# Score and state parts of two tiles in one 64-row visit, one-bank PSUM tiles, and a new fixed order of instructions

## The chip, the cores and the metric

The kernel runs on one core of one Trainium2 chip. The time of a kernel is its device time in microseconds (us); a program is run several times, and the median counts. The kernel before took 214.94 us (median of three runs, 214.93 to 215.87).

## What is computed

Inputs are q, k, v with 4 batches, 8 heads, 768 positions and head size 64, a gain vector of 512, and two weight matrices (512 x 2048 and 2048 x 512). The first part is a recurrence per batch and head; the second a normalised two-layer network with a residual:

```python
for t in range(S):
    state = gamma[None, :, None, None] * state + np.einsum('bhd,bhe->bhde', k[:, :, t], v[:, :, t])
    y[:, :, t] = scale * np.einsum('bhd,bhde->bhe', q[:, :, t], state)
...
mu = np.mean(x, axis=-1, keepdims=True)
var = np.mean((x - mu) ** 2, axis=-1, keepdims=True)
xn = (x - mu) / np.sqrt(var + 1e-06) * g_ln
ch = np.maximum(xn @ w_ch1, 0.0) @ w_ch2
return (x + ch).astype(np.float32)
```

Here x is y with the heads side by side, so one position has 8 x 64 = 512 features.

## The kernel before, in words

**Tiles.** The work is cut into 24 tiles of 128 positions. Tiles 0 to 3 are the first chunks of the four batches; tiles 4 to 8 are chunks 1 to 5 of batch 0, tiles 9 to 13 those of batch 1, and so on. Per tile the recurrence is done in chunk form. The steps, with their names in the code:

- Loads `k`, `q`, `v`: GpSimd (POOL) issues them with a cast to bf16 (L430). From tile 8 (`T0 = 8`) q and k lie side by side in one buffer.
- Before tile 8, TensorE (PE) transposes k and q with an identity (L498, L505), 4 instructions each, ScalarE (ACT) copies kT out (`ek`) and VectorE (DVE) scales qT (`eq`, L510). From tile 8, one DMA transpose issued by SyncE (SP) turns q and k together (`tr`, L520), and DVE scales qT (L527).
- Scores `pa` (L538): 8 matmuls that contract over 64 rows of the array, for the 8 heads, even heads on rows 0 to 63 and odd heads on rows 64 to 127. They write `pa`, one tile over two PSUM banks.
- DVE multiplies the scores by the decay mask (`asb`, L562) in one instruction of 1024 columns.
- The state part: q times the state of earlier chunks. For tiles 4 to 7 it is 4 full-height matmuls (L582) inside `py`; from tile 8 it is 8 matmuls of 64 rows (`ps`, L548), which come just before the tile's scores. Scores and state parts together are a "visit" of the array in 64-row form.
- `py` (L572, L586): 8 matmuls of masked scores times v. From tile 8 even and odd heads go to two banks, b1 and b2.
- The state: POOL scales v (`vg`, L633), PE multiplies kT by it into bank `pd` (L645), DVE scales the result into one of two state buffers (`pb`, L659).
- DVE takes mean and variance (`bn`, L601), normalises (`xn`, L613), ACT keeps a copy of y (`xc`, L619). xn is transposed on PE for tiles 0 to 7 (`tx`, L672, copied out by ACT as `ex`) and by a DMA transpose on SP from tile 8 (`ex`, L686).
- Network: `m` (L719) is a first-layer unit with 512 PSUM columns; groups have 1 tile (tiles 0 to 7), 2 tiles (8 to 15) or 4 tiles (16 to 23), so a matmul has 128, 256 or 512 columns. `r` is the relu that empties it, on ACT (L732) or DVE (L734). A unit uses one of two `mm` banks. The second layer (L757, "m2") takes 16 matmuls of 512 columns per tile in a bank b0, b1 or b2; DVE adds the residual (L767) and ACT issues the store (L774).

**PSUM.** Eight banks: `pd` 1, `mm` 2, `pa` 2, b0, b1, b2.

**Order.** No scheduler runs at compile time: `ORDER` (L29) is a list of task numbers written out by hand, and `Plan.order` walks it, so each engine's queue has exactly this order. Every engine takes its queue in order, and waits at an instruction whose inputs, or whose buffer, aren't ready. A plan's cost figures (the `a(...)` calls) only place filler matmuls on zeros (`warm`, L785) in the first 14 us. POOL's queue also holds small copies (L447), which wait for an earlier load to land and so pace the loads.

Of the kernel before, what the change touches and what calls it, by code (L numbers as in the profile page):

```python
# [14 lines left out]
PE, ACT, DVE, POOL, SP = range(5)  # L15

CFG = {
    "T0": 8, "TX": 8, "groups": [1] * 8 + [2] * 4 + [4] * 2,
    "first": ["iota", "pos", "v0", "k1", "q1", "v1", "w1_0", "k2", "q2", "w1_1", "v2",
              "k3", "q3", "v3", "w1_2", "k4", "q4", "v4", "k5", "q5", "v5", "w1_3", "w2_0",  # L20
              "k6", "q6", "v6", "k7", "q7", "v7", "w2_1", "w2_2", "w2_3"],
    "bufs": {"qsb": 6, "ksb": 5, "vsb": 9, "qk": 8, "tr": 6, "vg": 3, "trq": 3, "trk": 3},
    "load_pad": 600, "w_pad": 550, "lead": 32, "lead2": 32, "sq_at": 28000, "late_load": 1700, "two": 4, "m2b": ("b0",), "m2all": 16, "inter": 4, "every": 4, "tail": (0, 384, 512), "step": 8, "pace": 8, "ahead": 3,
    "slack": 600, "tr_pad": 4000, "x_pad": 3500, "vg_pad": 2500, "fill": 0.8, "fill_end": 14000,
}

ORDER = [int(x) for x in """  # L29
16 17 2 0 3 19 20 23 14 8 15 1 24 5 7 9 25 4 10 6 13 21 11 26 18 45 22 27 146 28 149  # L30
100147 148 150 46 29 151 30 162 100163 153 12 152 165 154 164 166 155 31 156 157 167 32
158 168 169 47 100176 159 170 524 177 178 160 179 100172 214 180 181 171 173 532 33 215
182 183 525 184 534 161 190 533 193 34 35 36 526 100191 186 535 192 194 10527 187 540 37
38 185 542 195 48 196 49 39 541 216 197 204 40 42 43 41 536 198 50 217 543 207 234
100205 206 528 537 200 52 51 201 544 199 208 10529 224 209 545 552 188 548 10549 553 174
100225 210 227 550 551 546 53 55 175 226 228 211 54 212 44 218 219 547 213 554 530 220
555 251 202 221 235 100241 229 538 230 56 244 10531 236 556 539 242 275 231 558 100258
557 232 559 243 560 10561 237 562 57 245 246 233 238 239 563 222 566 259 564 247 260 567
248 189 261 570 262 252 565 568 249 60 254 255 250 569 223 253 203 263 100722 61 268 58
59 62 287 298 63 723 716 724 301 66 67 64 717 65 264 725 269 718 571 719 265 726 266 270  # L40
720 576 100271 276 307 267 578 272 579 577 728 273 68 69 278 277 72 729 730 731 318 73
279 70 299 71 280 580 572 732 281 300 282 74 322 284 286 734 735 75 288 581 283 285 736
302 303 290 289 573 737 291 738 574 319 584 292 740 741 293 320 294 296 742 308 304 240
585 78 575 743 582 744 295 297 310 333 79 76 309 77 339 586 305 583 311 80 746 587 334
747 312 335 313 314 274 316 323 81 315 748 84 350 749 351 588 592 317 325 85 82 83 379
750 589 256 257 324 354 326 727 602 86 752 87 753 327 328 329 603 593 590 754 755 594
591 330 90 331 340 352 332 342 756 341 343 721 380 598 321 599 595 91 758 336 759 344
760 761 596 733 88 345 89 355 762 346 368 348 353 600 92 757 745 739 337 597 347 93 764
96 349 97 94 381 601 95 765 98 338 357 604 356 766 606 386 99 605 382 607 767 358 306
359 383 614 612 768 360 384 615 361 613 363 770 397 102 771 103 100 362 772 398 365 364  # L50
763 369 101 104 371 370 773 403 610 372 608 774 611 373 776 616 609 399 366 105 374 387
108 109 617 375 618 414 367 377 106 107 777 620 418 751 376 378 389 619 110 388 778 390
779 622 415 391 385 404 780 392 393 621 623 630 782 395 111 114 429 115 631 394 112 400
456 113 433 626 116 624 117 396 406 120 121 416 405 430 783 627 625 407 784 431 408 628
419 409 634 785 410 629 632 411 412 457 118 119 122 413 421 635 786 445 633 420 123 788
126 458 422 127 789 646 124 423 424 790 425 427 647 401 125 426 428 791 642 638 434 436
792 435 794 795 796 639 643 465 769 437 438 640 417 439 440 442 128 797 459 641 129 441
446 443 476 132 644 798 432 402 133 645 636 130 448 447 648 131 134 138 637 460 650 449
450 649 800 651 461 451 452 801 802 477 454 803 444 775 480 462 453 466 478 455 135 491
804 136 137 468 492 467 806 139 495 807 469 470 140 493 808 471 141 809 472 142 474 473  # L60
475 652 653 654 481 483 482 484 810 655 656 658 143 510 479 485 144 787 506 805 657 799
145 659 660 661 486 662 507 496 487 489 664 663 488 508 490 666 498 497 665 499 667 668
670 669 500 671 501 502 672 673 504 511 812 674 503 505 676 513 512 675 514 678 463 677
680 515 679 682 813 681 814 683 516 494 811 509 517 781 519 464 518 520 815 100830 831
816 521 832 818 819 200824 820 825 684 817 793 685 826 690 688 691 827 689 694 696 833
695 522 686 697 687 708 709 821 698 699 692 693 523 822 848 700 828 834 702 100842 701
703 706 707 704 200836 714 837 705 715 712 838 849 843 713 710 711 850 844 845 839 846
851 840 100854 852 855 856 823 847 841 835 829 853 857 860 861 858 862 863 864 859 865
""".split()]


class Plan:

    def __init__(self, seen, begin, first_load):
        self.seen, self.begin, self.first_load = seen, begin, first_load  # L80
        self.tasks, self.bufs, self.chosen = [], {}, {}

    def pool(self, name, n):
        self.bufs[name] = n

    def add(self, eng, ns, rank, emit, after=(), takes=None, uses=(), load=0, hw=0, lat=0, at=0,
            follows=(), slack=0, slots=None):
        after = [d for x in after for d in (x if isinstance(x, list) else [x])]
        t = {"on": eng if isinstance(eng, dict) else {eng: ns}, "rank": rank, "emit": emit,
             "after": after, "takes": takes, "uses": list(uses) + ([takes] if takes else []),  # L90
             "slots": (slots or [(takes[0],)]) if takes else [],
             "load": load, "hw": hw, "lat": lat, "at": at, "follows": list(follows),
             "slack": slack}
        self.tasks.append(t)
        return t

    def order(self, seq):
        left, ends = {}, {}
        for t in self.tasks:
            for u in t["uses"]:  # L100
                left[u] = left.get(u, 0) + 1
        held = {name: [] for name in self.bufs}
        free = dict(self.begin)
        sw_free, hw_free, out = self.first_load, 0, []
        for number in seq:
            t = self.tasks[number % 10000]
# [55 lines left out]
def kernel(  # L162
# [9 lines left out]
):  # L172

    nc = tc.nc
# [641 lines left out]
```

## Time and profile before

| what | value |
|---|---|
| median time, 3 runs | 214.94 us |
| span of the profiled execution | 212.1 us |
| own time of the profiled execution | not given apart; the median is 2.9 us above its span |
| PE busy | 204.2 us (96%) |
| DVE, ACT, POOL busy | 121.6, 85.0, 95.8 us |
| granted TensorE clock | 1.000 |

The span runs from the first to the last instruction of the profiled execution; launch and end lie around it. Matmuls are pipelined: the duration that a row gives one matmul holds its way through the array, so the rate is read from the starts of rows, not from durations. A timeline row gives start, length, engine, line, what is written and read, shape and how many.

### The profile page before, as it was taken

Reading aid. Unit: us, or ns where it says so; the run is one execution under the profiler, and the core shown is the slowest. Engines: PE = TensorE matmul, PEld = TensorE weight load, DVE = VectorE, ACT = ScalarE, POOL = GpSimd, SP = SyncE. Lnnn points to the kernel's source line nnn. Section 1 sums busy time; section 2 is a strip of 40 time slices with the busy share of each in tenths; the row PEclk is TensorE's granted clock in tenths of the full one; section 3 lists DMA queues with packets and bytes.
Section 4 is the critical chain, followed back from the end, with each engine's and each line's share of the span. In section 5 each row is a group of like instructions: output and inputs, shape, how many; then the busy total and the mean of one; then the engine's idle time right before and its main releaser. Section 6 shows DMA issues by size and latency. Waiting matters only on the chain.

```text
span 212.1 us, 4939 instructions
## 1 busy us (share of the span) xinstructions
PE 204.2 (96%) x2005; PEld 130.8 (62%) x2027; DVE 121.6 (57%) x264; ACT 85.0 (40%) x173; POOL 95.8 (45%) x149
## 2 busy tenths in 40 slices
PE   7988999999999999999999999999999999999993
PEld 3468999975667666657576676574444444444442
DVE  6776778674566875664775777478676510030041
ACT  5485556750431323332352442351366601444200
POOL 8988697238776584657855837430000000000000
PEclk9999999999999999999999999999999999999999
DMA  9999999999999999999999999959440260000035
GB/s 130 174 180 180 163 198 173 208 139 114 112 100 93 155 119 177 168 269 145 134 145 181 105 173 84 157 83 151 86 157 10 65 185 3 0 0 0 0 141 209
DMA packets 108890, 26.85 MB, mean 127 GB/s; under 512 B 101569, under 2 KB 105921, under 8 KB 108866
## 3 DMA queue, kind: packets, MB, share of 16 engines
q0 software_dynamic: 77024, 13.37, 83.7%
q1 hardware_dynamic: 27186, 6.59, 21.1%
q10 hardware_dynamic: 4656, 6.56, 9.0%
q8 instruction: 16, 0.26, 0.5%
q14 instruction: 8, 0.07, 0.1%
HBM read 27.30 MB, written 6.29 MB: 158 GB/s over the span
## 4 chain that ended last, share of the span: by engine, by line
PE 87%; DMA 8%; POOL 3%; issue 1%; DVE 0%; POOLq 0%
PE b L757 39%; PE mm L719 38%; DMA ksb<-in_k_dram 4%; DMA w<-in_moe_w_ch_dram 3%; PE pa L538 2%; PE pd L645 2%; PE b L572 2%; PE b L548 2%; POOL v L430 1%; PE b L498 1%; PE b L672 1%; POOL vg L633 0%; PE b L586 0%; PE b L582 0%; PE b L505 0%
## 5 line engine op out<-in xcount | busy, mean ns | idle before, releaser
L719 PE MATMUL mm<-xnt,w 128*128 128x128 bf16 (+2 forms) x896 | 95.5, 257 | 0.2 <-ACT xnt L256 0.2
L757 PE MATMUL b<-w,h 128*128 128x512 bf16 (+2 forms) x379 | 88.4, 370 | 1.2 <-issue 0.2
L732 ACT ACTIVATE h<-mm 128x512 bf16<-128x512 f32 x91 | 53.8, 599 | 81.4 <-PE mm L719 81.1
L719 PEld LDWEIGHTS <-w 128*128 128x128 bf16 x896 | 66.0, 98 | 20.5 <-issue 0.2
L757 PEld LDWEIGHTS <-h 128*128 128x128 bf16 x400 | 37.1, 98 | 37.7
L562 DVE TENSOR_TENSOR asb<-pa,mask 128x1024 bf16<-128x1024 f32 x24 | 29.4, 1224 | 19.9 <-PE pa L538 19.7
L767 DVE SCALAR_TENSOR_TENSOR osb<-b,rstd,x_all 128x512 f32<-128x512 f32 (+2 forms) x25 | 18.0, 726 | 25.9 <-PE b L757 25.6
L601 DVE BATCH_NORM_STATS2 bns<-b 128x6 f32<-128x256 f32 (+1 forms) x40 | 17.8, 477 | 17.7 <-PE b L572 10.9
L619 ACT CAST x_all<-b 128x256 bf16<-128x256 f32 (+1 forms) x40 | 16.2, 416 | 22.5 <-DVE xn L613 20.3
L613 DVE SCALAR_TENSOR_TENSOR xn<-b,mv,gb 128x256 bf16<-128x256 f32 (+1 forms) x40 | 20.1, 532 | 0.7
L633 POOL TENSOR_TENSOR vg<-vsb,vsc 128x512 bf16<-128x512 bf16 x16 | 16.6, 1044 | 6.7 <-PE pd L645 5.9
L430 POOL DMA_DIRECT2D vsb<-in_v_dram x20 | 18.0, 901 | 2.7 <-issue 1.6
L659 DVE TENSOR_TENSOR state<-pd,gch 64x256 bf16<-64x256 f32 x40 | 16.6, 415 | 4.1 <-PE pd L645 3.2
L430 POOL DMA_DIRECT2D qk<-in_k_dram x16 | 14.3, 892 | 2.6 <-issue 2.0
L430 POOL DMA_DIRECT2D qk<-in_q_dram x16 | 14.2, 890 | 0.7 <-issue 0.7
L447 POOL COPY scrap<-qk 1x1 bf16<-1x1 bf16 x30 | 5.4, 181 | 13.4 <-DMA qk<-in_k_dram 11.7
L447 POOL COPY scrap<-vsb 1x1 bf16<-1x1 bf16 x15 | 2.6, 177 | 16.4 <-DMA vsb<-in_v_dram 16.3
L700 DVE RECIPROCAL rstd<-rstd 128x1 f32<-128x1 f32 (+2 forms) x14 | 2.2, 157 | 12.9 <-ACT rstd L694 12.8
L785 PE MATMUL pd<-zeros 128*128 128x512 bf16 (+1 forms) x24 | 6.6, 420 | 1.3 <-DVE zeros L291 1.2
L438 POOL DMA_DIRECT2D w<-in_moe_w_ch_dram x8 | 6.2, 776 | 3.0 <-DMA w<-in_moe_w_ch_dram 3.0
L572 PEld LDWEIGHTS <-asb 128*128 128x128 bf16 x128 | 5.8, 98 | 2.4
L527 DVE TENSOR_TENSOR trq<-tr,qsc 128x512 bf16<-128x512 bf16 x16 | 6.9, 432 | 0.0
(68 smaller groups left out, 127.9 us busy)
## 6 DMA issues: line engine op xcount, KB each, us to landing
out_dram<-osb ACTq DMA_DIRECT2D x23, 256.0 KB, 3.2
w<-in_moe_w_ch_dram POOLq DMA_DIRECT2D x8, 512.0 KB, 10.0
vsb<-in_v_dram POOLq DMA_DIRECT2D x20, 128.0 KB, 5.4
qk<-in_k_dram POOLq DMA_DIRECT2D x16, 128.0 KB, 4.7
qk<-in_q_dram POOLq DMA_DIRECT2D x16, 128.0 KB, 4.9
qsb<-in_q_dram POOLq DMA_DIRECT2D x7, 128.0 KB, 9.1
v<-in_v_dram POOLq DMA_DIRECT2D x4, 128.0 KB, 7.0
ksb<-in_k_dram POOLq DMA_DIRECT2D x4, 128.0 KB, 9.5
```

The source lines that it names most:

```text
L430: nc.gpsimd.dma_start(out=tile_of(kind, j), in_=src)
L562: nc.vector.tensor_tensor(out=take("asb", t, [P, NPAIR, 2, P], BF16).rearrange("p i a t -> p a i t"), in0=held["pa", t], in1=mask.rearrang ...
L572: nc.tensor.matmul(half_y[h % 2][:, h // 2 * D:(h // 2 + 1) * D], lhsT=held["asb", t][:, h // 2, h % 2, :], rhs=tile_of("v", t)[:, h, :], ...
L601: nc.vector.bn_stats(out=bns[:, t, i, :], in_=x)
L613: nc.vector.scalar_tensor_tensor(out=dst, in0=src, scalar=mv[:, t, 0:1], in1=g, op0=ALU.subtract, op1=ALU.mult)
L619: nc.scalar.copy(out=dst, in_=src)
L633: e.tensor_tensor(out=take("vg", j, [P, H, D], BF16), in0=tile_of("v", j), in1=vsc[:, cc, :].unsqueeze(2).to_broadcast([P, H, D]), op=ALU. ...
L659: nc.vector.tensor_tensor(out=held["pb", n][o, :, o], in0=held["pd", b][o, :, o], in1=gch[o, cc, :].unsqueeze(2).to_broadcast([D, NPAIR, D ...
L719: nc.tensor.matmul(p[:, j, :], lhsT=w1[:, ko, (ho + j) * P:(ho + j + 1) * P], rhs=held["xnt", hb][:, h0:h0 + n, ko, :], start=(ko == 0), s ...
L732: nc.scalar.activation(out=dst, in_=src, func=AF.Relu)
L757: nc.tensor.matmul(held[key][:, 0:w], lhsT=held["h1", hb][:, ho, i * P:(i + 1) * P], rhs=w2[:, ho, cols], start=(ho == 0), stop=(ho == HO ...
L767: nc.vector.scalar_tensor_tensor(out=take("osb", key, [P, w], FP32), in0=held[key][:, 0:w], scalar=rstd[:, t:t + 1], in1=x_all[:, t, cols] ...
```

## The change

The kernel is written anew around the same steps; the order is now a list of named tokens. A token is a step and its tile (`eq8`, `py8`), for `m` and `r` a group and its first hidden block (`m8_0`), for `z` (second layer) a tile and a quarter (`z3_2`); after a slash stand the engine, and after a second one the PSUM banks. `vis8` is the visit of tiles 8 and 9; `am9b` is the mask product of tile 9's odd heads; `gk9` and the like are POOL's pacing copies, `W` and `Z` the weight loads, `ad` and `st` residual and store.

- From tile 8 on, tiles go in pairs: one visit holds the scores of both tiles, 16 matmuls, and then the state parts of both, 16 matmuls. There are 8 visits instead of 16 there.
- PSUM is eight one-bank tiles: X0 to X3 shared by first-layer units and scores (a pair takes all four), Y0 and Y1 for even and odd heads of the pair's y, M for transposes and second-layer tiles, PD for the state. Near the end second-layer tiles also use Y0, Y1 and PD.
- The mask product is one DVE instruction per bank (512 columns), two for each tile.
- `T0` goes from 8 to 6: tiles 6 and 7 are transposed by DMA, and their state parts are done in 64 rows.
- Three state buffers instead of two; a second-layer quarter waits for its own quarter of w2 only.
- A new order throughout. The matmul of the gain vector (`gb`) now precedes tile 0's transposes; more of the early relus are on DVE.

```diff
-    "T0": 8, "TX": 8, "groups": [1] * 8 + [2] * 4 + [4] * 2,
+CFG = {'T0': 6,
+ 'pairs': [(8, 9), (10, 11), (12, 13), (14, 15), (16, 17), (18, 19), (20, 21), (22, 23)],
...
-            ("pd", 1, ps), ("mm", 2, ps), ("pa", 1, ps),
-    BANKS = ("b0", "b1", "b2")
+    BANK = {name: ps.tile([P, 4 * P], FP32, name=name)
+            for name in ("X0", "X1", "X2", "X3", "Y0", "Y1", "M", "PD")}
...
-            for i in range(NPAIR):
-                for par in range(2):
-                    o = slice(D * par, D * (par + 1))
-                    nc.tensor.matmul(
-                        half_y[par][:, i * D:(i + 1) * D], lhsT=held["trq", t][o, i, :],
-                        rhs=held["pb", t][o, i, o], start=(i == 0), stop=False)
+    def _(eng, first):
+        ts = visit[first]
+        for t in ts:
+            for i in range(NPAIR):
+                for par in range(2):
+                    o = slice(D * par, D * (par + 1))
+                    nc.tensor.matmul(bank(("pa", t, par))[:, i * P:(i + 1) * P], lhsT=kT(t)[o, i, :],
+                                     rhs=slot(trq, t)[o, i, :], start=True, stop=True)
+        for t in ts:
+            for i in range(NPAIR if t >= T0 else 0):
+                for par in range(2):
+                    o = slice(D * par, D * (par + 1))
+                    nc.tensor.matmul(
+                        y_of(t, par)[:, i * D:(i + 1) * D], lhsT=slot(trq, t)[o, i, :],
+                        rhs=slot(state, chunk(t) - 1)[o, i, o], start=(i == 0 and t == ts[0]), stop=False,
+                        skip_group_check=True)
...
-                out=take("asb", t, [P, NPAIR, 2, P], BF16).rearrange("p i a t -> p a i t"),
-                in0=held["pa", t],
-                in1=mask.rearrange("p (i a) t -> p a i t", a=2), op=ALU.mult)
+            out=slot(asb, t)[:, :, par, :], in0=bank(("pa", t, par)).rearrange("p (i t) -> p i t", t=P),
+            in1=mask.rearrange("p (i a) t -> p a i t", a=2)[:, par], op=ALU.mult)
...
+m2_12//X2 tr7 m4_12//X3 tx5//Y1 m1_12//X0 r2_12/D gq8 ex5 xc5 v7 Z1 m4_4//X2 r4_12/A eq6 Z2 vg6
+m5_0//X1 z1_0//M r4_4/A r1_12/A Z3 vis6//X3,X2 r5_0/A m5_8//X0 am6a am6b k8 pd6 m4_0//X3 q9 py6
...
+tr8 bn7 xn7b xn7a gv8 k9 vg1 xc7a xc7b r6_0/A sq6 r6_8/A r6_12/A q10 z2_0//Y0 z0_0//Y1 z2_1 v9
+pb8 r4_8/D ad1 rs0 rs2 tx7//M tr9 gk9 k10 ex7 pd1 z0_1 m7_0//X0 z2_2 z2_3 z0_2 gq10 q11 gv9 v10
+vg9 tr10 z0_3 z3_0//M ad2 eq8 pb9 ad0 gk10 k11 r7_0/A sq5 z3_1 eq9 gq11 gv10 pd9
+vis8//X2,X1,X3,X0 v11 q12 z3_2 am9b am9a am8a z3_3 tr11 gk11 k12 ad3 gv11 am8b py9 m6_4//X0
+m7_4//X3 py8 vg10 st3/A r7_4/A gq12 r6_4/A q13 z4_0//M v12 z4_1 rs4 pb10 bn8 rs5 bn9 z4_2 xn9a
+xn8b z4_3 xc8b gk12 ad4 k13 pd10 gv12 vg11 rs6 xn8a xn9b pb11 eq10 eq11 ex9 m7_8//X3 m7_12//X0
+z5_0//M v13 xc9a r7_8/A r7_12/A sq7 xc8a xc9b z5_1 ex8 gk13 vg12 vis10//X1,X2,X3,X0 gq13 k14
+tr12 z5_2 am11a am11b z5_3 tr13 gv13 q14 vg2 v14 py11 pd11 am10b ad5 m8_0//X2 z6_0//M bn11 am10a
...
```

## Prediction

> **What bounds the kernel now.** I read the page's busy table first, then the chain of work that ended last, then a timeline of TensorE alone. The page:
>
> ```profile
> PE 204.2 (96%) x2005; PEld 130.8 (62%) x2027; DVE 121.6 (57%) x264; ACT 85.0 (40%) x173; POOL 95.8 (45%) x149
> PEclk9999999999999999999999999999999999999999
> PE 87%; DMA 8%; POOL 3%; issue 1%; DVE 0%; POOLq 0%
> ```
>
> TensorE is busy all the time at full clock, and the chain is TensorE's own queue for 87% of the span; the DMA and POOL shares belong to the start, where loads gate the first tiles. The busy time by stretch of the steady part says the same (columns: stretch, PE, PEld, DVE, ACT, POOL busy, clock, DMA share, GB/s):
>
> ```profile
> 24.00:206.00 182.00, 180.79 (x1734) 114.71 (x1753) 102.61 (x211) 70.89 (x145) 75.63 (x121) 1.00 1.09 119
> ```
>
> From 24 us on, 180.8 of 182 us are covered. I also compared the start of each matmul with the one before: after 23.2 us nearly every matmul starts one streaming time after its predecessor (0.056, 0.109 or 0.216 us for 128, 256, 512 columns), bar records that the trace lost, one pause of 0.2 us at 97 us, and the visits in 64-row form. One visit, in the timeline of TensorE:
>
> ```profile
> 131.04 1.91 PE L719 MATMUL mm<-xnt,w 128*128 128x256 bf16 x16
> 132.88 0.29 PE L548 MATMUL b<-state,trq 64*128 64x64 bf16 x8
> 133.01 0.39 PE L538 MATMUL pa<-trq,tr 64*128 64x128 bf16 x8
> 133.33 2.76 PE L757 MATMUL b<-w,h 128*128 128x512 bf16 x11
> 135.93 0.40 PE L572 MATMUL b<-vsb,asb 128*128 128x64 bf16 x8
> 136.16 1.04 PE L719 MATMUL mm<-xnt,w 128*128 128x256 bf16 x8
> 137.03 1.03 PE L757 MATMUL b<-w,h 128*128 128x512 bf16 x4
> ```
>
> The 8 matmuls from 136.16 to 137.03 take 0.87 us, 0.109 each. At that rate the 16 from 131.04 are through at 132.78, but the visit starts at 132.88: 0.10 us is lost on entry. The 8 scores take 0.32 us to the next start; even and odd heads overlap, so they stream 4 x 128 columns, 4 x 0.056 = 0.22 us: 0.10 us is lost on leaving. **So one visit costs about 0.2 us beyond its work.** Everything that TensorE no longer does is time won, if nothing arrives late.
>
> **The Trainium skill.** "TensorEngine Tiling (Array Packing)", Key Properties, says that a change of tiling mode drains the TensorEngine. The two pauses of 0.10 us are that; the page has no price. "TensorE: Matmul & The Clock Gate", Back-to-back issue gap, gives N/2.4 + 2.5 ns warm: 56, 109 and 216 ns, as here. "PSUM — Partial Sum Buffer", in its section on bank collisions, says to guard PSUM by bank and quadrant: a mask product per bank frees each bank alone, but scores in a bank keep first-layer units out of it; no run here shows the mixed use. "DMA: Bandwidth & Descriptors", Queues, rings and completion order, says that the DMA engines go round their queues packet by packet: transposes and loads take from each other. The trace agrees: score transposes land 3.0 to 7.0 us after issue, later while loads are dense.
>
> **The change part by part,** against the profiled execution: span 212.1 us; its own time isn't given, and the median is 2.9 us above the span. I leave that as it is.
>
> Removed from TensorE, all on the bounding queue:
>
> ```profile
> 28.97 0.39 PE L505 MATMUL b<-idn,qsb 128*128 128x128 bf16 x4
> 29.20 0.39 PE L582 MATMUL b<-state,trq 128*128 128x128 bf16 x4
> 29.42 0.40 PE L586 MATMUL b<-vsb,asb 128*128 128x64 bf16 x8
> ```
>
> 1. Transposes of q and k of tiles 6 and 7: 4 groups of 4; a group takes 29.20 - 28.97 = 0.23 us. **-0.9 us.**
> 2. State parts of tiles 6 and 7: full-height 0.22 us (29.42 - 29.20), in 64 rows 0.13 us (133.01 - 132.88), inside visits that exist anyway: 2 x 0.09, **-0.2 us.**
> 3. Eight visits fewer, 0.2 us each: **-1.6 us.** Bounds: 0.1 us each if only entry or leaving is saved (-0.8), and 0.25 if the small 64-row work also packs better over two tiles (-2.0). I take 0.2, since a merged visit has one entry and one leaving.
>
> Sum -2.7; with roundings I take **-2.6 us.** All other matmuls keep number and shape.
>
> Edits that I cost at nothing, with their cover. **Mask product per bank:** 48 of 512 columns for 24 of 1024 (1224 ns). The nearest row is VectorE's relu of 512 columns, 687 ns; below, half of the old, 612. That is 0 to 3.6 us more on VectorE, busy 57%. For a pair of tiles it has about 4 x 0.65 mask, 2 x 0.75 residual, 4 x 0.42 state, 4 x 0.48 normalising, 4 x 0.42 + 2 x 0.21 statistics, 2 x 0.43 scaling, 10.6 us by these durations (they overlap by nearly 0.1 when back to back: about 9) in 11 to 14 us of TensorE work from visit to visit. It fits, and the first product starts half a microsecond earlier. If the cover is gone, the rest of the visit's banks come late (rival A). **ACT copies of kT** for tiles 6 and 7 go away; ACT isn't bound. **The start:** the gain matmul, 1.05 us, moves ahead of tile 0's transposes and delays them, and the same 1.05 us is gone behind its scores. Afterwards TensorE waits for loads anyway (k of tile 2 lands at 12.7, k of tile 4 at 23.1 us), and POOL's queue up to w1's last load holds the same loads, with the first `vg` one load later or earlier. In the new order 8.7 us of TensorE work lie between the k transposes of tiles 2 and 4, for 10.4 us of time. So tile 4 begins at 23.2 us as before: 0, within 0.4 either way. **The end:** the same last tile in 384 + 128 columns, 0.
>
> Added waits. I added up TensorE's work along the new order, starting from 23.2 us at tile 4's k transpose, and held it against arrivals:
>
> ```profile
> L520 SPq DMA_TRANSPOSE tr<-qk x16: 1231/1242/2214, 46.9 to 147.3; - x16
> DMA to landing us min/median/max: 3.0/5.1/7.0
> L686 SPq DMA_TRANSPOSE xnt<-xn x16: 1189/1192/1886, 68.5 to 169.4; - x16
> DMA to landing us min/median/max: 2.4/3.9/7.2
> ```
>
> - **`tr6`, new on SP's queue:** q of tile 6 landed at 34.7 us before; the transpose is issued at about 34.3, lands 5.1 later, plus scaling 0.43: ready at about 40. `vis6` comes up on TensorE at 39.5. Late by 0 to 2 us; I take **+0.5.** All TensorE work stands behind it.
> - **w2:** POOL now takes q8, v6, a pacing copy that waits for q8 (about 38.5 us), and v7 before three of w2's four loads. Four loads at about 2.5 us apart then land near 44.5, 47 and 49.5; the quarters `z1_1`, `z1_2`, `z1_3` come up at 45.3, 47.8, 49.8. On time by a few tenths; late by up to 1.5. I take 0.
> - **`tr9`:** k9's load stands behind pacing copies on k8, q9, v8 and can't land before about 56; transpose 5, scaling 0.4: 61.4 against `vis8` at 61.8. Up to 1.5 late. I take 0.
> - **`ex8` before `m8_0`:** by the same addition VectorE ends the pair's last normalising 5 us before the unit comes up; SP issues `ex9` first (1.2), so `ex8` has 3.8 us, and landing has median 3.9, up to 7.2. 0 to 2 late; I take **+0.4.** `m12_7` has the same form late in the kernel (3.9 us after `ex19`); loads are thin there and xnt then lands in 2.4 to 3. I take 0.
>
> A pause lets the later arrivals catch up, so they don't simply add. Sum: -2.6 + 0.9 = **-1.7: 213.2 us.**
>
> **Rivals.**
> A. *The four X banks become the bound (slower).* A pair visit needs all four banks empty, and no first-layer unit can start until mask products free them. After `vis8` TensorE has two second-layer quarters, 1.73 us, then `py9`; two mask products take 1.3. Then two units in X0 and X3, 1.8 us, cover the rest. For: covers are that short at every visit, and scaling of both tiles, two states and the bank's relus must now all be done at once. Against: VectorE has 2 us to spare per pair, and relus are done 0.6 us after their unit. If each of 8 visits waits x, the gain is gone at x = 0.33 (2.6/8), and it is slower by over 0.5% (1.07 us) at 0.46. At 0.6 it is 214.94 - 2.6 + 4.8 = 217.1.
> B. *Transposes and w2 arrive late (no change).* Late `tr6` 1.0, w2 0.5, `ex8` 1.1: 2.6 us, **214.9.** For: landing spreads over 5 us. Against: loads per time are as before, and waits overlap.
> C. *The change doesn't save the drains:* two tiles' work in one visit meets pauses inside, at the border of tiles or of scores and state parts. Then only 1 and 2 remain: -1.1 + 0.4 late, **214.2.** Against: state part to scores shows no pause today (0.13 us for 4 pairs of 64 columns).
>
> **Chances.** 0.5% is 1.07 us, about what a measurement can tell from no change: bounds 213.87 and 216.01. Forecast (212.2 to 213.8) 0.61; B 0.19; C 0.06; A 0.14. Faster: 0.61, and a bit of C's upper end: 0.62. Same: the rest of B and C, 0.24. Slower: 0.14. Range 212.1 (no wait at all and 0.2 more) to 216.2 (into A's lower end); some 0.12 of A and a few hundredths below lie outside.
>
> **What would show it.** Right: 64-row entries in the timeline from tile 8 fall to 8, each costing about 0.1 us in and out; no transposes of tiles 6 and 7 on PE; TensorE's starts close-packed after 24 us, apart from pauses under 1 us ahead of `vis6` and `m8_0`, ended by DMA. Wrong: pauses ended by VectorE or ACT after each visit (A), pauses ended by DMA of over 2 us in sum (B), visits longer than about 0.95 us (C), or a lower clock after a pause.

## The result, and the profile after

The changed kernel took **221.74 us** (median of 4 runs, 219.36 to 224.56) beside 215.41 us for the kernel before on the same chip (4 runs, 214.93 to 216.29): a ratio of **1.027, 95% interval 1.020 to 1.034, slower.** The forecast was 213.2. The profiled execution of after took 221.75 us, its span is 220.0 us, 7.9 more than that of before. Here and below, some executions of every kernel run a few per cent longer than the others; the ratios leave these out and the medians don't, so the two can differ a little.

The page of after, busy times and clock:

```profile
PE 208.6 (95%) x2025; PEld 132.3 (60%) x2025; DVE 134.3 (61%) x313; ACT 68.1 (31%) x153; POOL 97.6 (44%) x149
PEclk9999999999999997999999999999999999999998
```

VectorE has 12.7 us more and ScalarE 16.9 us less than before: work has gone from one to the other. One slice of the clock inside the run, the 16th of 40 (82.5 to 88 us, 5.5 us each), is below full. By stretch, with the columns of before:

```profile
24.00:206.00 182.00, 177.32 (x1768) 114.66 (x1766) 113.06 (x251) 58.38 (x133) 77.91 (x121) 0.99 1.08 117
```

Only 177.3 of 182 us are covered, where it was 180.8; and some of that cover is matmuls at half clock. TensorE's waits, with what ended them (total, times, longest, us):

```profile
PE X L394 <- DVE trq L385: 2.1, 4, 1.4
PE PD L459 <- POOL vg L451: 1.3, 1, 1.3
...
PE X L506 <- DMA xnt<-xn: 1.0, 1, 1.0
PE X L506 <- DVE xnt L245: 0.5, 1, 0.5
PE X L327 <- DMA grow<-in_moe_g_ln_dram: 0.5, 1, 0.5
```

The waits are few, and no one of them explains 8 us. To see where time is lost I lined the trace up with the order: for each step, its start less the streaming time of all matmuls ahead of it (0.056, 0.109 or 0.216 us each, 0.2 for a visit). I call that the **lag**. A kernel that never waits has a constant lag; the rounding of these prices leaves some tenths of a us over the whole kernel. Tile 4 of the kernel before has 5.65.

```
step (start us, lag)        after           e16 (best version, below)
k of tile 4             26.28   8.76        23.44   5.93
visit 5                 32.70   9.35        29.35   6.00
second layer, tile 3    64.02   9.85        61.67   6.41
visit 8                 66.54  10.41        63.72   6.51
visit 10                79.09  10.84        75.78   6.44
unit 8_0                84.68  13.32        81.04   6.86
second layer, tile 7    95.73  15.00        88.68   6.86
visit 12                98.42  15.10        91.37   6.96
visit 18               141.87  15.04       134.82   6.91
visit 20               153.78  16.44       145.29   6.87
last quarter           216.24  16.25       207.78   6.71
```

So the loss is in five places: the start (3.1 us over before), visit 8 (1.0: 0.6 ahead of it and 0.4 inside), the state of tile 11 and unit 8_0 (2.5), a stretch after that (1.6), visit 20 (1.4), with about 1.0 in small steps between. From visit 12 to visit 18 the lag stands still.

**The merged visit** itself, in TensorE's timeline of after:

```profile
77.70 1.46 PE L529 MATMUL M<-w,h 128*128 128x512 bf16 x6
79.09 0.62 PE L394 MATMUL X<-trq,tr 64*128 64x128 bf16 x16
79.55 0.40 PE L400 MATMUL Y<-state,trq 64*128 64x64 bf16 x16
79.87 1.47 PE L529 MATMUL M<-w,h 128*128 128x512 bf16 x6
```

Six matmuls of 0.216 from 77.70 end at 79.00: 0.09 on entry. Sixteen scores take 0.46 to the state parts (8 x 0.056 = 0.45, no pause between the tiles), those 0.32 for 8 x 0.028 = 0.22: 0.10 on leaving. So one visit of two tiles is entered and left at the price of a visit of one tile.

**The start**, same view:

```profile
5.28 2.04 PE L327 MATMUL X<-grow,ones 1*128 1x512 f32 x2 [0.49 <-DMA grow<-in_moe_g_ln_dram]
...
7.86 0.63 PE L371 MATMUL Y<-idn,k 128*128 128x128 bf16 x4
...
20.75 1.05 PE L506 MATMUL X<-xnt,w 128*128 128x128 bf16 x16 [0.52 <-DVE xnt L245]
...
22.69 0.38 PE L480 MATMUL Y<-idn,xn 128*128 128x128 bf16 x4 [0.44 <-DVE trk L245]
```

The gain matmul waits for its own load and takes 2.04 us where it took 1.12 before, since the clock is still at half (the 4 transposes behind it take 0.43 us to the next start, 0.107 each for 0.056); tile 0's transposes, which began at 4.61, begin at 7.86. And `trk` and `xnt`, the copies out of PSUM, come from VectorE (L245), no longer from ScalarE: their tokens name no engine, and the helper's default is VectorE. Fourteen copies of 0.41 us moved.

**Visit 8**, all engines:

```profile
63.22 2.09 DVE L385 TENSOR_TENSOR trq<-tr,qsc 128x512 bf16<-128x512 bf16 x1
63.96 1.05 POOL L451 TENSOR_TENSOR vg<-v,vsc 128x512 bf16<-128x512 bf16 x1
...
66.22 0.38 PE L459 MATMUL PD<-vg,qk 128*128 128x128 bf16 x4 [0.32 <-DVE state L469]
...
67.25 0.40 PE L394 MATMUL X<-trq,tr 64*128 64x128 bf16 x8 [0.31 <-DVE trq L385]
```

The transposed q of tile 8 had landed at 55.56 and that of tile 9 at 63.09, so neither transpose is waited for here. VectorE's scaling of tile 8's q, 0.42 us elsewhere, takes 2.09 us beside a product on POOL and ends 0.3 us after it. It holds back the state behind it in VectorE's queue, for which TensorE waits ahead of the visit, and then the scaling of tile 9's q, for which the visit pauses between its two tiles.

**Tile 11's state and unit 8_0.** POOL's queue, then TensorE's:

```profile
70.88 0.18 POOL L365 COPY scrap<-v 1x1 bf16<-1x1 bf16 x1 [0.50 <-DMA v<-in_v_dram]
...
75.42 0.18 POOL L365 COPY scrap<-qk 1x1 bf16<-1x1 bf16 x1 [3.37 <-DMA qk<-in_q_dram]
...
82.09 0.18 POOL L365 COPY scrap<-v 1x1 bf16<-1x1 bf16 x1 [2.88 <-DMA v<-in_v_dram]
82.23 1.03 POOL L451 TENSOR_TENSOR vg<-v,vsc 128x512 bf16<-128x512 bf16 x1
```

```profile
83.31 0.38 PE L459 MATMUL PD<-vg,qk 128*128 128x128 bf16 x4 [1.30 <-POOL vg L451]
84.68 1.04 PE L506 MATMUL X<-xnt,w 128*128 128x256 bf16 x8 [0.98 <-DMA xnt<-xn]
85.55 3.58 PE L529 MATMUL M<-w,h 128*128 128x512 bf16 x8
88.92 1.07 PE L506 MATMUL X<-xnt,w 128*128 128x256 bf16 x8
```

The product `vg11` (82.23) has had its v since 70.76 (where the copy at 70.88 was released), but stands in POOL's queue behind the pacing copies for q12 (75.42) and v12 (82.09). TensorE waits 1.30 us for it, then 0.98 for `ex8`, whose transpose was issued at 78.32 and landed at 84.54. The first hides part of the second: in e2 below, `vg11` is there in time, and TensorE waits 2.3 us for `ex8` alone. Then 8 matmuls of 512 columns take 3.37 us from start to start, 0.42 each, twice 0.216: half clock, 1.6 us lost.

**Visit 20**, all engines:

```profile
151.29 2.05 POOL L451 TENSOR_TENSOR vg<-v,vsc 128x512 bf16<-128x512 bf16 x2
151.43 2.21 DVE L385 TENSOR_TENSOR trq<-tr,qsc 128x512 bf16<-128x512 bf16 x1
...
153.78 0.62 PE L394 MATMUL X<-trq,tr 64*128 64x128 bf16 x16 [1.37 <-DVE trq L385]
```

The scaling of q takes 2.21 us here, beside two products on POOL, and ends 0.3 us after the second.

### The profile page after: what moved, and what is told of

It reads as the page before. It is cut to its first block, busy times and chain, and to the rows that moved or that the text cites. A ratio compares the mean times of both kernels' runs of the same rounds, so it can differ in the third digit from the quotient of the medians.

```text
span 220.0 us, 4981 instructions
## 1 busy us (share of the span) xinstructions
PE 208.6 (95%) x2025; PEld 132.3 (60%) x2025; DVE 134.3 (61%) x313; ACT 68.1 (31%) x153; POOL 97.6 (44%) x149
## 4 chain that ended last, share of the span: by engine, by line
PE 77%; DVE 15%; DMA 4%; issue 1%; SPq 0%; ACT 0%; DVEq 0%; ACTq 0%
PE X L506 33%; PE M L529 20%; PE Y L529 11%; PE PD L529 3%; DMA xnt<-xn 3%; DVE trq L385 3%; DVE xn L440 3%; PE X L394 2%; PE Y L422 2%; DVE bns L430 2%; DVE asb L407 2%; DVE state L469 2%; DMA grow<-in_moe_g_ln_dram 2%; PE PD L459 2%; DVE h L519 1%
## 5 line engine op out<-in xcount | busy, mean ns | idle before, releaser
L506 PE MATMUL X<-xnt,w 128*128 128x128 bf16 (+2 forms) x896 | 94.0, 257 | 1.8 <-DMA xnt<-xn 1.0
L517 ACT ACTIVATE h<-X 128x512 bf16<-128x512 f32 x85 | 48.3, 602 | 113.4 <-PE X L506 112.6
L529 PE MATMUL M<-w,h 128*128 128x512 bf16 x240 | 59.2, 387 | 0.0
L407 DVE TENSOR_TENSOR asb<-X,mask 128x512 bf16<-128x512 f32 x48 | 30.5, 681 | 8.6 <-PE X L394 8.4
L529 PE MATMUL Y<-w,h 128*128 128x512 bf16 (+2 forms) x128 | 26.7, 352 | 0.0
L336 POOL DMA_DIRECT2D v<-in_v_dram x24 | 21.7, 904 | 2.8 <-issue 2.1
L430 DVE BATCH_NORM_STATS2 bns<-Y 128x6 f32<-128x256 f32 (+1 forms) x41 | 17.1, 450 | 9.4 <-PE Y L422 7.9
L451 POOL TENSOR_TENSOR vg<-v,vsc 128x512 bf16<-128x512 bf16 x20 | 21.3, 1065 | 3.1 <-PE PD L459 1.9
L440 DVE SCALAR_TENSOR_TENSOR xn<-Y,mv,gb 128x256 bf16<-128x256 f32 (+1 forms) x41 | 19.4, 508 | 0.5
L469 DVE TENSOR_TENSOR state<-PD,gch 64x256 bf16<-64x256 f32 x40 | 16.7, 417 | 4.3 <-PE PD L459 4.0
L365 POOL COPY scrap<-qk 1x1 bf16<-1x1 bf16 x30 | 5.7, 190 | 23.2 <-DMA qk<-in_q_dram 13.1
```

The lines of the kernel that those rows point to most:

```text
L336: nc.gpsimd.dma_start(out=dst, in_=tok[kind][TILES[t]])
L407: nc.vector.tensor_tensor(out=slot(asb, t)[:, :, par, :], in0=bank(("pa", t, par)).rearrange("p (i t) -> p i t", t=P), in1=mask.rearrange( ...
L430: nc.vector.bn_stats(out=bns[:, t, i, :], in_=x)
L440: nc.vector.scalar_tensor_tensor(out=dst, in0=src, scalar=mv[:, t, 0:1], in1=g, op0=ALU.subtract, op1=ALU.mult)
L451: nc.gpsimd.tensor_tensor(out=slot(vgs, chunk(t)), in0=v_of(t), in1=vsc[:, c, :].unsqueeze(2).to_broadcast([P, H, D]), op=ALU.mult)
L469: nc.vector.tensor_tensor(out=slot(state, chunk(t) - 1)[o, :, o], in0=pd[o, :, o], in1=gch[o, c - 1, :].unsqueeze(2).to_broadcast([D, NPAI ...
```

## The experiments

Each ratio is that to the kernel before, run beside it, with its 95% interval. Tokens are those of the order; `/A` puts a copy on ScalarE.

**First, the two parts of the start, and the scaling.** The theory was that the start and the later waits add up, so a repaired start is kept; the rival that loads set the later times.

`e1_copies_on_act`, the 14 copies back on ScalarE:

```diff
-ek0 ... ek5, ex0 ... ex7
+ek0/A ... ek5/A, ex0/A ... ex7/A
```

> The changed kernel, with the PSUM copies of kT (tiles 0 to 5) and of the transposed xn (tiles 0 to 7) back on ScalarE. In the changed order their tokens name no engine, and the copy routine then takes VectorE. Theory (the start is lost to VectorE, which got 14 copies of 0.41 us, and to the gain matmul, which waits for its load ahead of tile 0): tile 4's k transposes start at about 24.7 us instead of 26.3, and the time falls by 1 to 1.6 us, less where a load-bound wait at 83 us swallows it. Rival (the four X banks bind after each visit): the start moves, but the time stays within 0.5 us.

Measured: 220.53 us, ratio 1.026 [1.018, 1.034]. Tile 4 begins 1.2 us earlier than in after and tile 3's second layer 2.3 us earlier (lag 7.51 for 9.85), but visit 8 only 0.6 (65.97) and unit 8_0 0.3 us (84.37). The gain was there and was taken back by waits for what POOL makes of late loads: the state of tile 9, ahead of visit 8, waits 2.08 us for the product of v9, which POOL begins at 64.54, behind its pacing copy for v9 (63.20) and one more load, and the state of tile 11 waits 2.80 us for `vg11`.

`e2_gain_late`, the gain matmul behind tile 0's scores, as before:

```diff
-vsc hqc0b/A hkc0/A warm8_0 gb//X1 warm1_2 tk0//Y1 hqc0a/D qsc gl ek0 tq0//M W0 eq0 mask k2
-warm4_1 vis0//X2,X0 q2
+vsc hqc0b/A hkc0/A warm8_0 warm1_2 tk0//Y1 hqc0a/D qsc ek0 tq0//M W0 eq0 mask k2
+warm4_1 vis0//X2,X0 gb//X1 gl q2
```

> The changed kernel, with the gain matmul and its copy put back behind the scores of tile 0. Theory: tile 0's k transposes start at about 5 us instead of 7.9, since nothing waits for the gain vector's load any more; tile 4's at about 25, the time falls by about 1 to 1.5 us. Rival (loads gate the start anyway, as I predicted): tile 4's transposes stay at 26.3 us, within 0.4, and so does the time.

Measured: 220.24 us, 1.024 [1.018, 1.031], span 216.8. Tile 4 is 0.4 us earlier. Visit 8 has no wait or pause, since the scaling ahead of it takes 0.41 us (1 us less lag), and the half clock after 8_0 is absent (1.7 us; clock 1.000), though TensorE waits 2.3 us there. So most of the shorter span doesn't come from the start itself.

`e3_copies_and_gain`, both:

> Both of the former together. Theory: tile 4's k transposes at 23.2 to 23.5 us, as in the kernel before; time down by up to 3.1 us against the changed kernel, by 1.5 or more if the later waits for loads take back a part. Rival (X banks): start as said, time unchanged.

Measured: 221.86 us, 1.033 [1.027, 1.039]. No gain at all. Tile 4 begins at 25.20, not at 23.2 to 23.5: the copy of k0, behind that of q0, holds TensorE for 0.9 us, and the loads of k of tiles 2 and 3 and of q of tile 3 for 1.1. Visit 6 now waits 1.4 us for tile 6's scaled q, and visit 8 begins at 66.92 and 8_0 at 85.79, as late as in after. In four kernels with four starts, visit 8 begins between 65.7 and 66.9. **In e1 and e3 the rival holds: what arrives then sets these times** (in e3 the state of tile 9 waits 1.47 us for the product of v9, begun at 65.50). TensorE's lateness at the start had hidden the lateness of the loads.

`e4_scale_fp32`, the scale factors in four bytes, on the thought that a product of 2-byte operands alone shares something with POOL:

```diff
-    qsc = sb.tile([P, NPAIR, P], BF16, name="qsc")
+    qsc = sb.tile([P, NPAIR, P], FP32, name="qsc")
```

> The changed kernel, with the scale that multiplies qT kept in fp32 instead of bf16, so that VectorE's product of tr and scale has operands of mixed width. Theory (in five of 18 cases this product took 0.7 to 2.2 us instead of 0.42 because a product of v on GpSimd ran beside it, and both bf16 operands make it use something the two engines share): every one of the 18 takes the same 0.6 to 0.7 us, none above 0.8, though GpSimd's products still overlap some; the wait of TensorE before the visit at 153.8 us falls from 1.4 us to under 0.5, the time falls by 1 to 2 us. Rival (the long ones wait for the transposed q to land, and the profile books the wait as duration): long ones stay as they are.

Measured: 221.38 us, 1.028 [1.019, 1.038]. Durations min/median/max in ns:

```profile
L385 DVE TENSOR_TENSOR trq<-tr,qsc x18: 640/684/1557, 42.2 to 164.1; 128x512 bf16<-128x512 bf16 x18
```

The median rose by 0.27 us and long ones remained: 1.30 and 1.56 us beside a `vg`, 1.43 us at 42.2, ahead of one. My thought fell: a wider operand doesn't avoid it. Nor does the rival hold, that the wait for a late transpose is booked as duration: in after the two longest scalings, at 63.22 and 151.43, had their q since 55.56 and 148.61.

**Then, what the loads stand behind.** `e5_w2_first` is e3 with the pacing copy on q8 moved behind w2's loads, where the kernel before lets them go:

```diff
-... m1_12//X0 r2_12/D gq8 ex5 xc5 v7 Z1 ... vg7 v8 gk8 gq9
+... m1_12//X0 r2_12/D ex5 xc5 v7 Z1 ... vg7 v8 gq8 gk8 gq9
```

> The kernel with kT copies on ScalarE and the gain matmul late, and in addition GpSimd's first pacing copy (it waits for q8 to land) put behind the loads of w2, k8, q9 and v8, as in the kernel before. Theory (from 45 to 85 us the loads, which pace one another through the copies on GpSimd, set the time; in the changed order GpSimd stands idle for 5 us at the first pacing copy, with three loads of w2 behind it): k9 lands at about 50 us instead of 58, visit 8 no longer waits for tr9, and what the two repairs of the start won is kept up to there: visit 8 starts at about 64 us instead of 66.5; time 1.5 to 2.5 us below that of the two repairs alone. Rival (the transposes of tiles 6 and 7 need that pause; without it they land late): visit 6 waits 2 us more, and nothing is won.

Measured: 226.71 us, 1.052 [1.042, 1.061]; 5 us slower, not faster. `tr6` is issued at 35.83 among those loads and lands 13.3 us later, `tr7` 16.7; visit 6 waits 8.3 us. So the pause had a reason: **with it w2 and everything behind is late, without it tiles 6 and 7 are.**

`e6_plus_tile8_late` adds `vg11` ahead of the pacing copies, and unit 8_0 two quarters later:

```diff
-py8 vg10 st3/A r7_4/A gq12 ... gk12 ad4 k13 pd10 gv12 vg11
+py8 vg10 st3/A r7_4/A vg11 gq12 ... gk12 ad4 k13 pd10 gv12
-ad5 m8_0//X2 z6_0//M ... gk14 r8_0/A k15 eq12 z6_1 m8_10//X0
+ad5 z6_0//M ... gk14 k15 eq12 z6_1 m8_0//X2 r8_0/A m8_10//X0
```

> The former, and in addition: the product of v11 on GpSimd before the pacing copies for q12 and v12, and the first-layer unit 8_0 behind two quarters of tile 6's second layer. In the changed kernel TensorE waits 1.3 us at the state of tile 11 for that product, which stands behind a copy that waits for v12, then 1.0 us for the transposed xn of tile 8, and then runs at half clock for 3.4 us. Theory: both waits shrink to under 0.7 us in sum and the half clock goes; 3 to 4 us less than the former. Rival (one late thing only moves): TensorE waits as long at the next use of loads, and less than 1 us is won.

Measured: 225.58 us, 1.049 [1.040, 1.057]. From visit 8 to the second layer of tile 7 the lag grows by 0.6 us (15.83 to 16.39), where it was 4.6 in after: both waits and the half clock are gone there. Visit 6 still waits 6.5, visit 20 1.5 us.

`e7_no_pacing`, e3 without any pacing copy (`gk`, `gq`, `gv` taken out):

> The kernel with kT copies on ScalarE and the gain matmul late, without any of GpSimd's pacing copies: each load is issued as soon as its buffer is free. Theory (loads through the copies set the time between 45 and 85 us): k9 lands before 52 us, visit 8 and unit 8_0 wait less; but the DMA transposes share the engines with more loads, so they land 6 to 10 us after issue instead of 3 to 6, and waits move there. Time within 2 us of the two repairs alone, either way. Rival (X banks bind): waits stay where they are, after the visits.

Measured: 228.70 us, 1.065 [1.057, 1.073]. Visit 6 begins at 48.31, and the lag grows again at 8_0 (to 20.0) and by visit 18 (to 23.2). Most of the loss is again visit 6 (8.4 us, as in e5). What the other pacing copies are worth isn't clear of noise: e5, which only moved the one on q8, took 226.71, and the intervals overlap.

`e8_split_visits`, e6 with each pair's visit in two, second-layer matmuls at full height between them:

```diff
-        for t in ts:
-            for i in range(NPAIR if t >= T0 else 0):
+        if len(ts) == 1:
+            state_part(ts)
+        else:
+            late.append(ts)
...
+            if late and token[:3] != "vis" and token[0] in "zmp" and token[:2] not in ("pb", "po"):
+                state_part(late.pop())
```

> The version with all repairs so far (copies, gain matmul, w2, tile 8), with each visit of a pair split in two: the scores of both tiles, then one group of full-height matmuls, then the state parts of both. That undoes the merging: 8 visits more. Theory (a visit costs 0.1 us on entry and 0.1 us on leaving): 1.6 us slower than the version with all repairs. Rival (drains of 64-row work cost nothing where the next weights are loaded ahead, and the merging won nothing): within 0.5 us.

Measured: 227.46 us, 1.056 [1.045, 1.065]. 1.9 us above e6 by the medians, but visit 6 waited longer too (8.1 us), so this pair proves little; the same split follows below on e9, which hasn't that wait.

**Next, undo the one part that needs the pause.** `e9_tiles67_on_pe` has tiles 6 and 7 transposed on TensorE again, and all repairs; `vg21` and `vg22` are parted as well, and k0 is copied ahead of q0:

```diff
-CFG = {'T0': 6,
+CFG = {'T0': 8,
...
-m2_12//X2 tr7 m4_12//X3 tx5//Y1 ... m4_4//X2 r4_12/A eq6 Z2 vg6 m5_0//X1
+m2_12//X2 tk6//Y0 ek6/A m4_12//X3 tq6//M eq6 tx5//Y1 ... m4_4//X2 tk7//Y1 ek7/A r4_12/A Z2 vg6 m5_0//X1 tq7//Y0 eq7
...
-ad11 gv21 gk21 ... gq22 v23 vg21 vg22 q23 gk22 k23
+ad11 gv21 vg21 gk21 ... gq22 v23 q23 gk22 k23 vg22
```

> Merged visits, one-bank tiles and the new order kept, but q and k of tiles 6 and 7 transposed on TensorE again (16 transposes and two full-height state parts more, 1.1 us), and all repairs: kT copies on ScalarE, the copy of k0 ahead of that of q0, gain matmul late, w2 loaded before the first pacing copy, the products of v11, v21 and v22 moved away from what they delayed, unit 8_0 later. Theory (the merging wins 1.6 us; what lost time is that DMA transposes of tiles 6 and 7 fall into the densest loading, so that either the transposes or, with a pause for them, w2 and all later loads come late): no wait over 1 us on TensorE after tile 4; time between 213 and 216 us, 5 us or more below every version so far. Rival (the merged visits themselves cost time, through the four X banks): waits after each visit, time over 218 us.

Measured: **214.52 us (14 runs), 0.996 [0.993, 0.999].** Tile 4 begins at 23.24 (lag 5.72), visit 8 at 63.52 (6.31). The profiled execution took 216.87 us, 2.4 above the median. It has two waits over 1 us that the theory had ruled out, 1.90 us at unit 9_0 and 1.28 at unit 12_7; apart from these it is read only up to visit 8.

`e10_tiles67_split` is e9 with e8's split:

> The former with each pair's visit split in two (scores of both tiles, one group of full-height matmuls, state parts of both), 8 visits more. Theory (0.1 us on entry and 0.1 us on leaving): 1.6 us slower than the former. Rival (merging wins nothing): within 0.5 us of it.

Measured: 215.84 us, 1.008 [1.005, 1.011]: 1.3 us above e9 by the medians, 2.6 by the ratios (0.012 x 214.7), whose intervals lie apart. TensorE's timeline:

```profile
75.72 0.62 PE L394 MATMUL X<-trq,tr 64*128 64x128 bf16 x16
76.27 1.04 PE L537 MATMUL M<-w,h 128*128 128x512 bf16 x4
77.24 0.41 PE L408 MATMUL Y<-state,trq 64*128 64x64 bf16 x16
77.58 1.04 PE L537 MATMUL M<-w,h 128*128 128x512 bf16 x4
```

Scores hold 0.55 us (0.45 and 0.10), the four matmuls between end at 76.27 + 0.86 = 77.13, and the state parts come 0.11 later and hold 0.34. Beside the whole visit that is 0.21 us more for one more entry. Eight of them: 1.7 us, inside what the times say. **The price of 0.2 us a visit is confirmed.**

`e11_tiles67_by_dma` has all of e9's repairs, but tiles 6 and 7 by DMA as changed:

> All repairs of the first of these four, but tiles 6 and 7 transposed by DMA as in the changed kernel; nothing else differs. Theory: visit 6 waits 5 to 8 us for its transposed q and k, which land 10 us or more after issue among w2's loads; 7 us or more slower than with TensorE's transposes. Rival (the start and the pacing were the trouble, not these transposes): within 1.5 us of it.

Measured: 226.80 us, 1.044 [1.037, 1.052], about 10 us above e9 by the ratios. Its start is clean (tile 4 at 23.34), and then:

```profile
39.40 1.03 PE L529 MATMUL M<-w,h 128*128 128x512 bf16 x4
48.68 0.61 PE L394 MATMUL X<-trq,tr 64*128 64x128 bf16 x8 [8.25 <-DVE trq L385]
```

```profile
L379 SPq DMA_TRANSPOSE tr<-qk x18: 1231/1242/5974, 35.5 to 160.8; - x18
DMA to landing us min/median/max: 3.0/5.2/16.8
```

Visit 6 waits 8.25 us, then TensorE runs at half clock to 52.8 us (16 matmuls of 128 columns from 49.43 to 51.11, 0.105 each for 0.056), 1.9 us more, and from visit 8 to the last quarter the lag stands still (16.81 to 16.92). The loss is in that one place: 8.25 + 1.9 us, the 10 us of the ratios.

`e12_only_tiles67_undone` is after with only tiles 6 and 7 on TensorE and the copy on q8 moved:

> The changed kernel as it is, with only this undone: tiles 6 and 7 are transposed on TensorE, and the first pacing copy, which made room for their DMA transposes, goes behind w2's loads. The copies on VectorE, the gain matmul ahead and the rest stay. Theory (that part costs most of what was lost after 45 us, the start the rest): k9 lands before 52 us, visit 8 doesn't wait for tr9; the waits at 83 us shrink; 3 to 5 us faster than the changed kernel, about 217 us. Rival: under 1 us.

Measured: 219.72 us, 1.020 [1.013, 1.027]: 2.0 us below after by the medians, 1.5 by the ratios, whose intervals overlap; less than I had thought. The start is as late as in after (tile 4 at 26.43). With the loads earlier, POOL begins `vg11` at 77.60 instead of 82.23, and neither the state of tile 11 nor 8_0 waits. But visit 10 pauses 1.22 us between its two tiles for a scaling that takes 2.15 us beside a product on POOL (in sum the lag grows from 10.05 to 11.39 up to 8_0), and visit 20 waits 1.6 us. So this part alone isn't the whole loss.

**Last, what each other repair is worth.** The first three undo one of e9's repairs each.

> The version with tiles 6 and 7 on TensorE and all repairs, with only this undone: the PSUM copies of kT (now tiles 0 to 7) and of the transposed xn are on VectorE again, as in the changed kernel. Theory (16 copies of 0.41 us on VectorE delay the first tiles; the later waits are gone, so the delay stays to the end): tile 4's k transposes about 1 us later than 23.2 us, 1 to 2 us slower in the end. Rival (VectorE has room in the start): within 0.5 us.

`e13_copies_on_dve` (`ek`, `ex` without `/A`): 215.71 us (20 runs), 1.002 [1.000, 1.005]. 1.4 us slower than e9 by the ratios, as the theory said. By visit 5 its lag is 1.3 us above e9's (7.06 for 5.80).

> The version with tiles 6 and 7 on TensorE and all repairs, with only this undone: the gain matmul ahead of tile 0's transposes and the copy of q0's half ahead of that of k0 on ScalarE, as in the changed kernel. Theory (TensorE waits for the gain vector's load, then runs a matmul[...] at half clock): tile 0's k transposes at 7.5 to 8 us, tile 4's 1.5 to 2.5 us later than 23.2, 1.5 to 2.5 us slower in the end. Rival (loads gate the start, as I predicted): tile 4's within 0.4 us of 23.2, and no slower.

`e14_start_as_changed` (gain early, q0's copy first): 216.40 us (20 runs), 1.002 [0.999, 1.005]. Its trace doesn't bear out a loss of that size: the gain matmul ran at full clock (1.09 us), tile 0's transposes began at 6.87 and tile 4's 0.3 us later than in e9. The two intervals just touch, so the price of this part stays open between 0.3 us, by the start of tile 4, and 1.3, by the ratios.

> The version with tiles 6 and 7 on TensorE and all repairs, without the moves of the products of v11, v21, v22 and of unit 8_0. Theory: the wait at the state of tile 11 and at unit 8_0 is back with 1 to 2.5 us, as is one of 1 to 1.5 us at the visit of tiles 20 and 21 or 22 and 23, where VectorE's product of tr and scale runs beside GpSimd's; 2 to 4 us slower. Rival (with loads early, both were repaired anyway): within 0.7 us.

`e15_no_tile8_repair` (`vg11`, `vg21`, `vg22`, 8_0 where the change has them): 216.50 us (14 runs), 1.003 [0.999, 1.007], 1.5 us slower than e9 by the ratios, under the 2 to 4 of the theory. From visit 10 to 8_0 the lag grows by 1.85 us (6.97 to 8.82), all of it a wait for `ex8`; `vg11` in its old place is in time, since the loads are early. At visit 20 it grows by 0.5, and right behind the state of tile 21 waits 1.70 us for `vg21`.

`e16_units_swapped` is e9 with later places for units that stand soon after their tile's DMA transpose (9_0 and 12_7, the two long waits in e9's trace); three later uses of bank X1 go to bank M with it:

```diff
-m9_0//X3 m9_8//X2 py12 ... m8_8//X0 ... m8_12//X3
+m8_8//X3 m8_12//X2 py12 ... m9_0//X0 ... m9_8//X3
...
-m12_7//X1 py20 ... z15_0//M
+z15_0//X1 py20 ... m12_7//M r12_7/A
```

> The version with tiles 6 and 7 on TensorE and all repairs, and in addition two first-layer units of tiles 10 and 11 change places with two of tiles 8 and 9, and the first quarter of tile 15's second layer (in bank X1) takes the place of unit 12_7, which comes later in bank M. Theory (TensorE's two longest waits there, 1.9 us at unit 9_0 and 1.3 us at unit 12_7, are for the transposed xn of tiles 11 and 19, which land 5 to 7 us after issue): both go, 2 to 3 us faster than without the swap, about 212 us, and faster than the kernel before. Rival (the late landing moves on to the next user): under 1 us.

Measured: **214.82 us (18 runs), 0.995 [0.992, 0.998]**, by the ratio as good as e9, not 2 to 3 us better: the two waits belonged to one execution of e9 (e10 waits 0.67 us at 12_7 and not at 9_0). The profiled execution of e16, one of its fastest, took 212.95 us, span 211.2:

```profile
24.00:206.00 182.00, 179.76 (x1739) 116.21 (x1761) 104.71 (x236) 63.80 (x141) 77.05 (x121) 1.00 1.10 122
```

Its lag grows by 0.8 us from tile 4 to the last quarter. This is the best version: by the ratio 0.5% faster than the kernel before (0.2 to 0.8%), by the medians over all executions only 0.1% (214.82 for 215.03), and by the quotient of the ratios (0.995 / 1.027) 3.1% faster than the change.

## Why the prediction was wrong, step by step

**The savings were right.** The price of a visit (0.2 us, bounds 0.1 to 0.25) is shown by e10 and e9, and by the visit in the trace. Rivals A and C fall: from visit 12 to 18 nothing is lost behind a pair's visit, and a visit whose inputs are there has no pause inside. What a merged visit adds is that it needs both tiles' scaled q: visit 8 of after and visit 10 of e12 paused between their tiles for the second one. The mask product per bank took 681 ns, inside the bounds given (612 and 687), and was hidden.

**Against the profiled execution of before** the sum said 212.1 - 1.7 = 210.4; the span is 220.0, 9.6 more. (By the medians the miss is 221.74 - 213.2 = 8.5. Time less span is 1.75 us in after; if it was that before, an estimate, the profiled execution of before took about 213.9 us, 1 us below its median.) From before's lag at tile 4 (5.65) to the last quarter of after (16.25) the lag rises by 10.6, of which the forecast had 0.9 as waits. That is the whole difference, to 0.1, and it comes from these steps:

1. **"The start: ... So tile 4 begins at 23.2 us as before: 0, within 0.4 either way"** failed by 3.1 us. The reason given, that "TensorE waits for loads anyway", was untested, and two things were missed. The gain matmul has a load of its own, which holds it until 5.28, and it ran at half clock in after (though not in e14, so that part differs from run to run). And I wrote of the kT copies only that ScalarE's "go away" for tiles 6 and 7: I did not see that 14 others change engine. e13 puts these at 0.6%. The waits for loads that I counted on do take up some delay: with only one of the two parts in place tile 4 is 0.3 us (e14) or 0.75 us (e13) later than in e9, with both 3.0.
2. **"`tr6` ... +0.5" and "w2 ... 0"** were costed one by one, though the same pause serves one and hurts the other. It lets `tr6` land on time (4.2 us after its issue) and holds back w2: its last three quarters land at 45.2, 48.3 and 51.8 us, against 39.2, 41.7 and 44.2 before, and k8 at 52.5 against 45.2. I had w2 landing near 44.5 to 49.5 and looked only at the quarters that use it; in after these were covered by TensorE's own lateness. The delay goes on down POOL's queue: e1 and e3 wait for the product of v9, and after waits for `vg11`, which in e12, with earlier loads, is in time. e5 and e11 show the other side, 8.3 us at visit 6. By the ratios of e9 and e11 the price of T0 = 6 without the pause is about 10 us; with it, 1.5 to 2 us, which is what e12 recovers, though not clear of noise.
3. **"`ex8` before `m8_0` ... +0.4"** was too small. `ex8` landed 6.2 us after its issue, within the spread stated (2.4 to 7.2), where the unit left it about 4. The wait in the trace is 1.0 us only because 1.3 us went by ahead of it (step 4); in e2 it is 2.3, in e15 1.7. The mechanism was right, the size was not: I took the median's wait, and it was the slowest of its kind in this execution.
4. **Missing from the list of waits**: POOL's product for tile 11 behind two pacing copies, 1.3 us. I had checked loads that stand behind a pacing copy, and not products. In after it hid behind the wait for `ex8`, so it cost little by itself; in e1 and e3 it is 2.80 us and the larger of the two. e6 shows that both go when `vg11` and 8_0 change place.
5. **Not priced: the half clock after a wait**, 1.6 us, although the prediction ends with "or a lower clock after a pause". The Trainium skill's "TensorE: Matmul & The Clock Gate", What's actually happening, ties half rate to an idle window of about 3.4 us. Here no single wait was over 1.3 us; two with 0.4 us of work between came ahead of it. At the same place e1 has the half clock after 2.80 and 0.24 us, but e3 doesn't after 2.80 and 0.70, nor e2 after a single 2.3. The trace decides: waits shorter than the page's window can be followed by half clock, and similar ones needn't be.
6. **Scaling "2 x 0.43"** for a pair holds only where POOL isn't multiplying: 2.21 us ahead of visit 20 and 2.09 ahead of visit 8, together 2.4 us of lag. The Trainium skill's "SBUF — State Buffer", Who interferes with whom, says that a VectorE instruction with two SBUF inputs contends with a GpSimd instruction that reads SBUF. The trace agrees, and e4 shows that a wider operand does not avoid it.

Undone one by one, the parts come to about 0.6% (e13), 0.6% (e14), 0.7% (e15) and 0.7% (e12 beside after), 2.6 of the 3.1% between after and e9; each of these has an uncertainty of half its size or more.

By its own sign, pauses ended by DMA of over 2 us in sum, rival B didn't show: in after these are 1.5 us, and most pauses are ended by VectorE or POOL, one step behind a load or beside a product. The statement that "a pause lets the later arrivals catch up, so they don't simply add" was right in one way only: e1 and e3 show that repairing the earlier of two losses yields nothing while the later one is set by loads. Rival B had late arrivals as its mechanism, with 2.6 us for its size.

**What stays open**: the share of the start order (e14), and how much of the half clock belongs to the change and how much to chance: the mean clock of the four executions of after was 0.989, 0.985, 0.999 and 0.991, and the one at 0.999 took 219.36 us. That w2 could be sent ahead of tile 6's q, so that neither waits, was not tried. And of the 1.6 us that the merging saves on TensorE, only 0.2 to 1.0 us shows in the times of e9 and e16 beside the kernel before (the interval of e16 reaches 1.6); where the rest goes in their usual executions isn't shown.

## What to carry to other kernels

An arrival that is late is invisible as long as TensorE is later still, so price a delayed queue by the absolute time of everything behind it, down to the last product or copy, and not just by the next user. Of two waits in a row, repair the one that ends last, or both: the other hides in it. When a DMA transpose moves into a stretch dense with loads, ask what a pause for it delays and what it costs without the pause; one of the two is paid. And where code gives an engine by a default, list each copy with its engine before and after.

## What the runs showed of the hardware

- DMA transposes of q and k took 3.0 to 8.5 us from issue to landing when loads were paced (after), and 12.6 to 16.8 us between w2's loads (13.3 and 16.7 in e5, 12.6 and 16.8 in e11).
- A product of two SBUF operands on VectorE that ran beside products on POOL ended about 0.3 us after them: 0.42 us became 1.05 (at 136.46 in after) or 2.09 us (at 63.22, begun ahead of it) beside one, and 2.21 us beside two.
- TensorE fell to half clock for 3.4 us after waits of 1.30 and 0.98 us, 0.4 us of work apart (after), and at the same place after 2.80 and 0.24 (e1), but not after 2.80 and 0.70 (e3) or one of 2.3 (e2).
- Entering or leaving the 64-row form costs 0.09 to 0.12 us each way, with one tile or two in the visit, and also when 4 matmuls at full height lie between.
